# Two layers of attention and gated mixing on one core: a third buffer for values, another order of projections at an even pace, and later weights' maxima and splits over more steps

## The chip, the cores and the metric

The kernel runs on one core of a Trainium2 chip. The core has five engines that work at the same time, each in the order of its own instruction stream: PE (TensorE, matrix products), DVE (VectorE), ACT (ScalarE), POOL (GpSimd) and SP (SyncE), whose queue here issues nearly all DMA transfers. They wait for each other through semaphores. The metric is the device time of one execution in microseconds (us); the median of three runs of the kernel before is 2376.07 us (2370.62 to 2380.80).

## The reference

Two layers, each an attention block A with a residual and a gated block B with a residual, run twice with the same weights. The sequence has 2048 rows of 640 columns, 32 heads of 20 columns, and 4 segments of 512 rows.

```python
# block A, x is the normalized input; phi(t) = t + 1 if t > 0, else exp(t)
q, k, v = x @ wq, x @ wk, x @ wv            # split into heads and segments
for s in range(4):
    p = softmax(q[s] @ k[s].T * scale + causal mask)
    a_dot = p @ v[s]
    a_mem = phi(q[s]) @ M / (phi(q[s]) @ z + 1e-6)
    outs.append(g * a_mem + (1 - g) * a_dot)
    M, z = M + phi(k[s]).T @ v[s], z + sum(phi(k[s]))
x = x + concat(outs) @ wo
# block B, x normalized again
z1, z2 = split(gelu(x @ w_in)); z2 = layernorm(z2)
x = x + (z1 * (w_sp @ z2 + b_sp)) @ w_out
```

## The kernel before

**Precision.** Products are exact to about fp32: each fp32 operand is scaled by a power of two and split into a high and a low fp16 part (`split_scaled`: an ACT instruction, line 84, for the high part, a DVE instruction, line 85, for the low one), and a product is three fp16 matmuls (high by high, high by low, low by high). The power of two comes from the largest magnitude in the matrix. For the weights needed later (wo, both halves of w_in, w_out) `other_scales` brings them from memory in 32 pieces (line 182), reduces each on DVE (line 184), transposes the column maxima on PE, and forms the scales in `pow2_max` and `pow2_spread` (lines 58 to 77, 195 and 196). `Weight.load` then brings a weight piece by piece once more, splits it, and stores both parts to memory (line 128). In the second layer these weights are made already, and `load` only brings the stored parts.

**Phases.** Per layer there are phase 1a (attention, `Attention.run`), phase 1b (output projection of the last rows, normalization, w_in; line 308) and phase 2 (mixing along the sequence and w_out). In layer 0's phase 2 the head of layer 1's attention is woven in (`early`).

**The attention loop.** Heads are taken in pairs, 16 pairs to a segment, 64 in all. A pair takes three steps, so that there are 192 steps (0 to 191), a lead of 10 before them and some behind; a segment is 48 steps. At each step `scores` forms a chunk of the scores twice on PE: once for the row maxima of a pair two ahead (tile `mp`, reduced on DVE at line 1248) and once, with the maxima already subtracted, for the exponentials (tile `es`, read by ACT at line 1241 into `P`). `cast` turns `P` into a high part on ACT (line 1258) and a low part on POOL (line 1259). `pvs` multiplies them by the values (line 1285), and `combine` divides and adds the memory's share. `maxes` transposes the row maxima on PE and sends them through DMA into rows of the operand tile `qk` (line 1271). `read` and `update` read and write the memory M.

**Dense work.** Between those run the projections, called dense work here: `value(t)` makes the values of 128 rows (30 matmuls, line 1009; ACT line 1014 and DVE line 1015 write them to the value tile), `unit(s, m)` makes queries and keys of one of five groups of heads of segment s (30 matmuls, line 1066), and `project(t)` makes 128 rows of the output projection (30 matmuls, line 1042). `prep(t)`, the preparation of 128 rows, loads and normalizes them (lines 208 to 211 and 988), splits them (ACT line 223, POOL line 224), and transposes them by DMA; it is issued 11 steps before the value that needs it.

**What sets the order.** PE's order is that of the program. `order` is a list of the dense work: `v4` is a value tile, `12` unit 2 of segment 1, `p3` an output tile. Each has a nominal PE time in ns (6480 for a unit, 4530 for the others), and `PACE` says how many ns of it may run per step from which step on; the function `step` turns accumulated work into steps. Background work (`background`: the maxima, then wo and the second half of w_in) is a generator that yields the step at which it is to go on; the streams are merged step by step, and what preparations and background issue is held behind the newest attention instruction of ACT, DVE and SP. Weight pieces are staged in the pool `abg`, which has two buffers.

**Values.** A value tile holds a segment's values, high and low part with a column of ones (128 x 4 x 32 x 41 fp16). There are two, segment s in tile s % 2, so a value of segment 2 cannot be written before the products of segment 0 are done.

## Time and profile before

| | |
|---|---|
| median of 3 runs | 2376.07 us |
| the profiled execution, its span | 2378.28 us, 2376.6 us |
| PE busy | 2189.4 us, 92% of the span |
| DVE busy | 1500.2 us, 63% |
| ACT busy | 1173.3 us, 49% |
| POOL busy | 983.8 us, 41% |
| attention loop, layer 0 (steps 0 to 191) | 112.4 to 644.8 us |
| attention loop, layer 1 | 1326.4 to 1831.1 us |

How to read it: PE is matmul, PEld the load of its weights, SPq an instruction of SP's queue. A row of a group gives line, engine, operation, the tile written <- the tiles read, the count, busy time and the mean in ns of one, and then the idle time of the engine ahead of it with what ended it. A row of waits reads "who <- for whom: total us, times, longest us". A row of the timeline gives start, duration, engine, line, operation and tiles. A row of a stretch gives start and end, length, busy time and count of each engine, the clock that PE was granted (1.00 is full), the busy share of the DMA engines and GB/s. A wait for several things is put down to the one that came last.

### The profile page before, as it was taken

Reading aid. Unit: us, or ns where it says so; the run is one execution under the profiler, and the core shown is the slowest. Engines: PE = TensorE matmul, PEld = TensorE weight load, DVE = VectorE, ACT = ScalarE, POOL = GpSimd, SP = SyncE. Lnnn points to the kernel's source line nnn. Section 1 sums busy time; section 2 is a strip of 40 time slices with the busy share of each in tenths; the row PEclk is TensorE's granted clock in tenths of the full one; section 3 lists DMA queues with packets and bytes.
Section 4 is the critical chain, followed back from the end, with each engine's and each line's share of the span. In section 5 each row is a group of like instructions: output and inputs, shape, how many; then the busy total and the mean of one; then the engine's idle time right before and its main releaser. Section 6 shows DMA issues by size and latency. Waiting matters only on the chain. (4 is left out here: it accounts for less than half of the span.)

```text
span 2376.6 us, 50474 instructions
## 1 busy us (share of the span) xinstructions
PE 2189.4 (92%) x20490; PEld 1304.8 (55%) x20490; DVE 1500.2 (63%) x2790; ACT 1173.3 (49%) x1452; POOL 983.8 (41%) x773
## 2 busy tenths in 40 slices
PE   5878899899899979999998889999998999999998
PEld 2445555556545535555554555656565555555655
DVE  7678868877754543544314678787766668545454
ACT  3278678877632221212112698887676334322221
POOL 2078678888710100100001598888777323000000
PEclk9999899999999989999999999999999999999999
DMA  5653535455553477976633436454453534887875
GB/s 158 161 145 97 131 102 139 111 157 131 148 161 100 112 228 196 231 210 178 184 72 113 90 86 173 106 132 102 123 165 107 145 87 110 250 216 185 221 205 123
DMA packets 509418, 350.17 MB, mean 147 GB/s; under 512 B 409280, under 2 KB 444224, under 8 KB 504064
## 3 DMA queue, kind: packets, MB, share of 16 engines
q1 hardware_dynamic: 509184, 346.93, 55.7%
q8 instruction: 161, 2.64, 0.5%
q14 instruction: 73, 0.60, 0.1%
HBM read 160.83 MB, written 97.93 MB: 109 GB/s over the span
## 5 line engine op out<-in xcount | busy, mean ns | idle before, releaser
L1259 POOL TENSOR_TENSOR PL<-P,PH 128x1280 f16<-128x1280 f32 x248 | 650.1, 2623 | 117.2 <-ACT PH L1258 106.4
L1248 DVE TENSOR_REDUCE mx<-mp 128x2 f32<-128x1024 f32 (+3 forms) x512 | 408.8, 817 | 106.9 <-PE mp L1204 105.4
L1241 ACT ACTIVATE P<-es,sc 128x1024 f32<-128x1024 f32 (+1 forms) x384 | 370.7, 965 | 142.5 <-PE es L1204 140.6
L1258 ACT CAST PH<-P 128x1280 f16<-128x1280 f32 x256 | 320.4, 1253 | 19.9 <-PE pv L1285 10.5
L308 PEld LDWEIGHTS <-th 128*128 128x128 f16 x1920 | 188.2, 98 | 172.8 <-issue 10.2
L662 PE MATMUL gp<-zh,wt 128*128 128x432 f16 x1024 | 235.5, 350 | 15.3 <-DMA wt<-wn 15.3
L662 PEld LDWEIGHTS <-wt 128*128 128x128 f16 x1536 | 151.3, 99 | 149.0 <-DMA wt<-wn 17.7
L1232 PEld LDWEIGHTS <-qk 60*128 60x128 f16 (+1 forms) x2048 | 91.4, 94 | 229.9 <-issue 157.6
L211 POOL TENSOR_TENSOR lnrs<-lnve,mhalf 128x1 f32<-128x1 f32 x92 | 56.7, 625 | 382.4 <-DVE lnve L210 379.9
L461 PEld LDWEIGHTS <-wt 128*128 128x128 f16 x1344 | 131.5, 98 | 112.6 <-DMA wt<-wn 0.2
L1232 PE MATMUL mp<-qk 60*128 60x512 f16 (+3 forms) x1024 | 138.8, 308 | 42.6 <-DVE mx L1248 41.6
L1232 PE MATMUL es<-qk 64*128 64x512 f16 (+3 forms) x1024 | 135.7, 301 | 37.4 <-ACT P L1241 25.4
L1204 PEld LDWEIGHTS <-big 64*128 64x128 f16 x3072 | 141.9, 96 | 51.2 <-issue 4.0
L1285 PE MATMUL pv<-vs,PH 128*128 128x41 f16 x2560 | 167.8, 183 | 2.1 <-DVE ab L1301 2.0
L1009 PE MATMUL vps<-wvh,xt 128*128 128x320 f16 x640 | 155.8, 310 | 13.9 <-DMA xt<-xnhl 11.9
L1285 PE MATMUL pv<-vs,PL 128*128 128x41 f16 x2560 | 163.8, 181 | 1.6 <-POOL PL L1259 1.6
L1285 PEld LDWEIGHTS <-PH 128*128 128x128 f16 x2560 | 142.6, 96 | 18.5
L308 PE MATMUL zp<-wi1h,th 128*128 128x432 f16 x640 | 149.0, 347 | 0.6 <-DMA th<-xnhl 0.6
L1285 PEld LDWEIGHTS <-PL 128*128 128x128 f16 x2560 | 143.4, 97 | 4.2 <-POOL PL L1259 2.1
L662 PE MATMUL gp<-zl,wt 128*128 128x432 f16 x512 | 137.3, 350 | 0.0
L1066 PE MATMUL kps<-xt,wkh 128*128 128x512 f16 x380 | 122.8, 393 | 9.2 <-DVE phl L1100 9.1
L1009 PEld LDWEIGHTS <-xt 128*128 128x128 f16 x960 | 91.4, 101 | 54.2 <-DMA xt<-xnhl 12.9
(248 smaller groups left out, 4342.1 us busy)
## 6 DMA issues: line engine op xcount, KB each, us to landing
wr<-in_B_w_sp_dram SPq DMA_DIRECT2D x32, 1024.0 KB
qk<-st SPq DMA_DIRECT2D x256, 120.0 KB
x<-x SPq DMA_DIRECT2D x56, 320.0 KB
z<-z SPq DMA_DIRECT2D x32, 432.0 KB
cz<-z SPq DMA_DIRECT2D x32, 432.0 KB
turned<-wt SPq DMA_DIRECT2D x24, 512.0 KB
wt<-turned SPq DMA_DIRECT2D x24, 512.0 KB
st<-qhl SPq DMA_DIRECT2D x40, 256.0 KB
```

The costliest lines, as they stand in the source:

```text
L308: nc.tensor.matmul(zp[:, n, :FHH], a[:, k, :], b[:, k, c:c + FHH], start=(k == 0 and j == 0), stop=(k == KD - 1 and j == 2))
L461: nc.tensor.matmul(o[:, :FHH], wt[:, x, m, :], zb[b][:, y, m, :], start=start and i == j == 0, stop=i == NP - 1 and j == 2, skip_group_che ...
L662: nc.tensor.matmul(gp[:, n, :FHH], wt[:, k % 2, a, k // 2, :], b[:, k, n * FHH:(n + 1) * FHH], start=(k == 0 and j == 0), stop=(k == NT - ...
L1009: nc.tensor.matmul(ps, a[:, k, c], b[:, k, n * 320:(n + 1) * 320], start=(i == 0), stop=(i == 14))
L1066: nc.tensor.matmul(ps, a[:, k, c], b[:, k, :], start=(i == 0), stop=(i == 14))
L1204: nc.tensor.matmul(out, g.big[r, 64 - 64 * s:192 - 64 * s], mk, start=False, stop=s == 1, skip_group_check=True)
L1232: nc.tensor.matmul(out[:, h, o:o + w], a[r, ac], b[r, bc], start=o == 0, stop=False, skip_group_check=True)
L1241: self.last_of["ACT"] = nc.scalar.activation(P[:, :, 512 * c:512 * c + ew], es[:, :, :ew], AF.Exp, scale=g.esc).ins
L1248: self.last_of["DVE"] = nc.vector.tensor_reduce(self.mx[m][:, :, i], mp[:, :, o:o + w], AX.X, ALU.max).ins
L1258: nc.scalar.copy(PH, P[:, h])
L1259: (nc.gpsimd if h == 0 or n < self.N - self.TAIL else nc.vector).tensor_tensor(PL, P[:, h], PH, ALU.subtract)
L1285: nc.tensor.matmul(pv[:, i, h, :], x[:, c:c + 128], v[:, j, h0 + h, :], start=(j == 0 and x is PH), stop=(j == i and x is PL), skip_group_ ...
```

## The change

Five edits, all in the attention phase:

- A third value tile (`self.vs[2]`, in a new pool). Segment s uses tile s % 3. Values of segment 2 can be written while segment 0 is read.
- Another `order`: the values of segment 2 (v8 to v11) are put between the units of segment 1 (between 10 and 14), those of segment 3 (v12 to v15) between the units of segment 2, and the first output tile p0 behind unit 24; p1 to p3 come one unit earlier.
- Another `PACE`: 960 ns per step from step 0 and 1050 from step 60 to the end, in place of 700 from step 0, 1150 from step 53 and 1250 from step 128. The dense work then ends at step 196.9 instead of 190.4.
- The maxima of the later weights: a piece every 1.7 steps from step -8 (0.75 before); the last steps of their reduction at 50, 56 and 62 (50, 51 and 53 before).
- The splits: wo from step 72 with 3 steps between a load and its split (55 and 1.3 before), the second half of w_in with its first split at step 108 and 3.5 steps between (69 and 3 before).

A bookkeeping set (`spent`) and an assertion come with it and issue nothing.

```diff
@@ other_scales
-    yield 51
+    yield 56
     dg = pow2_max(g, pool, psum, tag, g.wam, 3, 4)
-    yield 53
+    yield 62
     pow2_spread(g, psum, tag, dg, 3, 4)
@@ Attention.__init__
-        self.xt, self.vs = [self.xt, None], [self.vs, None]
+        self.xt, self.vs = [self.xt, None], [self.vs, None, None]
@@ value
-            def out(ps=ps.rearrange("p (h d) -> p h d", d=DH), v=self.vs[s % 2][:, t % 4, n * 16:(n + 1) * 16, :]):
+            def out(ps=ps.rearrange("p (h d) -> p h d", d=DH), v=self.vs[s % 3][:, t % 4, n * 16:(n + 1) * 16, :]):
@@ update, pvs
-        v = self.vs[s % 2]
+        v = self.vs[s % 3]
@@ run
-        PACE = (-LEAD, 2400), (0, 700), (53, 1150), (128, 1250), (END + G, 0)
-        order = "02 03 v4 04 v5 v6 v7 10 11 12 13 14 v8 v9 v10 v11 20 21 p0 22 23 24 v12 v13 v14 v15 30 31 p1 32 p2 33 p3 34 p4 p5 p6 p7 p8 p9 p10 p11".split()
+        PACE = (-LEAD, 2400), (0, 960), (60, 1050), (END + G, 0)
+        order = "02 03 v4 04 v5 v6 v7 10 v8 11 v9 12 v10 13 v11 14 20 21 v12 v13 22 v14 23 v15 24 p0 30 p1 31 p2 32 p3 33 34 p4 p5 p6 p7 p8 p9 p10 p11".split()
...
-                assert s < 2 or beg > G * (s - 1) + self.LV + 3, (i, beg)
+                assert s < 3 or beg > G * (s - 2) + self.LV + 3, (i, beg)
...
-                    yield -8 + 0.75 * i if _ is True else _
+                    yield -8 + 1.7 * i if _ is True else _
                 nc.sync.dma_start(g.bsp, self.b_sp.rearrange("(t p) -> p t", p=128))
-            yield 54
-            for j, (w, width, pace) in enumerate(((g.wo, D, 1.3), (g.wi[1], FHH, 3))):
+            yield 70
+            for j, (w, width, at, pace) in enumerate(((g.wo, D, 72, 3), (g.wi[1], FHH, 108, 3.5))):
                 w.tiles(g.top[j])
                 for i, _ in enumerate(w.load(self.bg, width, "bg")):
-                    yield 55 + 14 * j + pace * i
+                    yield at + pace * i
...
         g = self.g
+        self.vs[2] = values_tile(g, self.pool("avs", 1))
```

More of the change, by code (lines that the diff above doesn't have):

```diff
@@ L831, in __init__ @@
         self.last_of = {}
+        self.spent = {(0, 0), (0, 1)}
     def post(self, k, f, free=False):
@@ L858, in setup @@
         g, nc, tc = self.g, self.nc, self.tc
-        pool = lambda n, b, **k: ctx.enter_context(tc.tile_pool(name=n, bufs=b, reuse_waits="tile", **k))
+        pool = self.pool = lambda n, b, **k: ctx.enter_context(tc.tile_pool(name=n, bufs=b, reuse_waits="tile", **k))
         sk, self.p3, self.pl2 = pool("ak", 1), pool("a3", 2), pool("al2", 2)
@@ L987, in norm @@
             mv, rs = ln
+            assert s < 2 or self.spent.issuperset((s - 2, m) for m in range(NU)), t
             nc.vector.tensor_scalar(xt, xt, mv[:, 0:1], rs, ALU.subtract, ALU.mult)
@@ L1069, in unit @@
             self.out(nm, s, m, ps)
+        self.spent.add((s, m))
     def out(self, nm, s, m, ps):
@@ L1279, in pvs @@
         pv = self.pv[n]
-        v = self.vs[s % 2]
+        v = self.vs[s % 3]
         for i in range(4):
```

## The prediction

> **What bounds the kernel now.** I read, in this order: the page's span, busy time by stretch, the waits of the stretches that stand out, the timeline around the longest, and the groups for prices. The attention loop runs 192 steps per layer, three exponentials (L1241) per pair of heads, so counting L1241 tells the step.

> ```profile
> 112.40:232.90 120.50, 46.19 (x48) 0.96 0.48 122
> 232.90:321.90 89.00, 23.14 (x24) 0.86 0.55 134
> 321.90:644.80 322.90, 115.90 (x120) 0.99 0.50 129
> ```

> These are L1241 alone: start and end, length, ACT busy and its count, granted clock, DMA share, GB/s. They cut layer 0 into A (steps 0 to 47), B (48 to 71) and C (72 to 191). All instructions in the same stretches, then layer 1's A, B and C:

> ```profile
> core 0: us, PE busy (x) PEld busy (x) DVE busy (x) ACT busy (x) POOL busy (x), PEclk, DMA share, GB/s
> 112.40:232.90 120.50, 99.92 (x1495) 61.03 (x1494) 98.40 (x187) 97.45 (x124) 93.40 (x54) 0.96 0.48 122
> 232.90:321.90 89.00, 72.88 (x863) 47.67 (x861) 67.46 (x133) 58.46 (x77) 64.72 (x45) 0.86 0.55 134
> 321.90:644.80 322.90, 303.52 (x4255) 195.14 (x4256) 251.33 (x492) 253.40 (x316) 264.51 (x182) 0.99 0.50 129
> 1326.40:1435.80 109.40, 96.33 (x1495) 59.61 (x1494) 87.64 (x166) 97.04 (x124) 93.09 (x54) 1.00 0.35 88
> 1435.80:1504.40 68.60, 61.54 (x862) 40.55 (x860) 56.73 (x116) 53.81 (x72) 61.05 (x45) 1.00 0.63 173
> 1504.40:1831.10 326.70, 308.30 (x4255) 196.89 (x4254) 245.41 (x484) 248.87 (x307) 265.57 (x183) 0.97 0.48 123
> ...
> 112.40:177.40 65.00, 50.48 (x739) 31.76 (x737) 52.04 (x100) 47.51 (x62) 44.87 (x26) 0.92 0.56 143
> ```

> Both layers run the same matmuls (1495, 863 or 862, 4255), yet layer 0's B is 20.4 us longer than layer 1's and its A 11.1 us. The difference is the background work that only layer 0 does. C is bound by PE (94% busy in both); A is bound by nothing alone: in layer 1 PE 88%, ACT 89%, POOL 85%, DVE 80%. The last row is the first 24 steps of layer 0, 2.7 us each.

> The waits of layer 0's B, then two of its A, then the one of layer 1's A:

> ```profile
> ACT P L1241 <- PE es L1204: 15.4, 8, 6.1
> PE mp L1232 <- DVE mx L1248: 6.2, 7, 1.3
> PE es L1232 <- ACT P L1241: 6.0, 4, 2.9
> ACT woh L84 <- DMA wst<-in_A_wo_dram: 4.7, 3, 1.9
> ACT wi1h L84 <- DMA wst<-in_B_w_in_dram: 3.5, 1, 3.5
> PE wtp L58 <- DVE mr L1269: 2.3, 1, 2.3
> ```

> ```profile
> PE mp L1232 <- DVE mx L1248: 13.4, 13, 2.4
> DVE wap L184 <- DMA wmst<-in_B_w_in_dram: 5.4, 6, 1.6
> ```

> ```profile
> PE mp L1232 <- DVE mx L1248: 5.1, 10, 1.6
> ```

> In B, ACT waits in order for weight pieces that have not landed, the exponentials queue behind it, and PE waits for them. The reduction of the maxima adds a transpose (L58) that PE meets right behind the one of the row maxima. In A, DVE waits in order for the pieces whose maxima it takes, and the scores wait for DVE. The timeline shows the two worst places, on DVE, SP and ACT:

> ```profile
> 242.21 2.38 DVE L62 TENSOR_SCALAR wdg<-ident,wmx 4x4 f32<-4x4 f32 x1
> 250.09 2.35 DVE L196 TENSOR_SCALAR sc<-pw 128x2 f32<-128x2 f32 x1
> ```

> ```profile
> 303.88 0.40 SPq L128 DMA_DIRECT2D w_oh<-woh  x1
> 304.33 0.42 SPq L128 DMA_DIRECT2D w_ol<-wol  x1
> 304.79 0.92 SPq L123 DMA_DIRECT2D wst<-in_B_w_in_dram  x1
> ```

> ```profile
> 313.27 0.65 ACT L84 ACTIVATE wi1h<-wst,iv 128x432 f16<-128x432 f32 x1 [3.46 <-DMA wst<-in_B_w_in_dram]
> ```

> Two tiny DVE operations take 2.4 us each. The first piece of the next weight is issued behind the store of the finished one (1.6 MB) and lands 8.5 us later, with ACT standing before it for 3.5.

> **The change, part by part.** The sum is made against the profiled execution: 2378.3 us, of which the span is 2376.6. It is 2.2 us above the median of the three runs, so I take 2 off at the end.

> *Dense work (projections of values, queries, keys, outputs).* Its nominal PE time is written in the code: 4.53 us for a value or output tile, 6.48 for a unit. Rows for size, from the chain, and for what goes along:

> ```profile
> 1498.17 2.14 PE vps L1009 x15
> 1671.39 2.27 PE kps L1066 x10
> ```

> ```profile
> L1014 ACT ACTIVATE vs<-vps 128x320 f16<-128x320 f32 x64 | 28.0, 440 | 30.0 <-PE vps L1009 29.7
> L1015 DVE SCALAR_TENSOR_TENSOR vs<-vps,vs 128x320 f16<-128x320 f32 x64 | 30.5, 479 | 34.8 <-ACT vs L1014 34.8
> L988 DVE TENSOR_SCALAR xt<-xt,lnmv,lnrs 128x640 f32<-128x640 f32 x28 | 29.8, 1072 | 1.9 <-POOL lnrs L211 1.8
> L208 DVE BATCH_NORM_STATS2 lnst<-xt 128x6 f32<-128x320 f32 x56 | 24.4, 479 | 6.9 <-DMA xt<-x 6.8
> L224 POOL TENSOR_TENSOR xnhl<-xt,xnhl 128x640 f16<-128x640 f32 x28 | 40.2, 1436 | 65.3 <-ACT xnhl L223 62.2 <-PE mtp L1266 2.3 <-DMA qk<-st 0.8
> L1259 POOL TENSOR_TENSOR PL<-P,PH 128x1280 f16<-128x1280 f32 x248 | 650.1, 2623 | 117.2 <-ACT PH L1258 106.4
> L184 DVE TENSOR_REDUCE wap<-wmst 128x1 f32<-128x432 f32 (+1 forms) x31 | 20.6, 670 | 10.3 <-DMA wmst<-in_B_w_in_dram 6.7 <-DMA wmst<-in_B_w_out_dram 2.7 <-DMA wmst<-in_A_wo_dram 0.8
> ```

> Thirty value matmuls at 0.143 us are 4.3; thirty of a unit at 0.227 are 6.8, so the nominal units hold within 6%. By the paces, the dense work of A goes from 48 x 0.70 = 33.6 to 48 x 0.96 = 46.1 us (+12.5), B from 25.3 to 24.1 (-1.2), C from 56 x 1.15 + 62.4 x 1.25 = 142.4 to 120 x 1.05 = 126.0 (-16.4), and behind step 191, where there was none, stand 4.9 steps (+5.1). Nothing is added or removed. What moves into A are the values v8 to v10 and the preparations of v8 to v11; the third place for values lets them be written while segment 0 is still read.

> Layer 1, A: PE 96.3 + 12.5 = 108.8 us. At A's own PE share of 0.88 this takes 123.6 us, at C's 0.944 it takes 115.3; its density, 0.96 per step, lies halfway from A's 0.70 to C's 1.19, so I take 0.914: 119.0, **+9.6**. B: -1.2 at 0.90, **-1.4**. C: -16.4 at 0.944, **-17.4**. Behind step 191: between 0 (PE waits there for the last products anyway) and 5.4; **+3**. Layer 1: -6.2.

> Layer 0, A: here DVE decides. It has layer 1's 87.6, three values (6 x 0.479 = 2.9), four preparations (each 2 x 0.479 + 1.07 + some 0.34 of small ones, so 9.5), and the maxima. These are 32 pieces, of which at 1.7 steps apart 27 fall into A: 27 x 0.67 = 18.1. Together 118.1 us. At 0.82 (98.4 of 120.5, A now) this takes 144.6; the best share of DVE that I find over ten steps is this one, 0.905, and gives 130.5:

> ```profile
> 387.00:423.00 36.00, 32.15 (x420) 18.41 (x417) 32.59 (x63) 29.92 (x39) 30.49 (x22) 0.96 0.56 138
> ```

> Between them: a piece is now reduced 0.75 step (2.0 us) behind its issue, then 1.7 (over 4 us), so DVE's waits for pieces go (5.4 us above, and 2.7 for the last weight in L184's row). 98.4 of 120.5 - 8.1 is 0.875, which gives 135.0: **+14.5**. Ahead of step 0 seven maxima fewer, 4.7 us of DVE beside a chain of projections: 0 to -4, **-2**.

> Layer 0, B: of its 20.4 us excess over layer 1, wo's splits (five, to steps 72 to 99) and the first of wi1 leave it altogether; the reduction stays, at steps 56 and 62 for 51 and 53. Step 56 has no transpose of row maxima before it, as step 51 has, so the 2.3 us before L58 go; the two DVE operations of 2.4 us stay. Layer 1's B would be 67.2; I add 4 for them and get 71.2, **-17.8**. Bounds: 67.2 (-21.8), or the whole excess of B's first 12 steps stays, 9.5 us (42.2 us in layer 0, 32.7 in layer 1, by L1241), giving 76.7 (-12.3).

> The clock is 0.86 in this stretch and 1.00 in layer 1's, 12.5 us of its 89, although PE's longest wait in it is the 2.9 us quoted. [...]

> Layer 0, C: -16.4 at 0.94, -17.4. Six splits move in (0.65 to 0.83 us of ACT each, less than 1.1 on DVE) where ACT and DVE are 78% busy: hidden, as long as each piece has landed. A split now comes 3 or 3.5 steps (8 us) behind its issue instead of 1.3. The store of wo still has the first piece of wi1 behind it, at step 99, but that one is split at 108; what remains is the fetches of queries and keys and the rows of maxima queued on SP behind 1.6 MB. Between 0 and the 3.5 us above; **+3** with wi1's own, larger store at step 174. So **-14.4**. Behind step 191: PE idles more there than in layer 1; **+1.5**. Layer 0: -2 + 14.5 - 17.8 - 14.4 + 1.5 = -18.2.

> The preparations that go into A hold a DVE scalar operation (L988, 1.07 us on average) beside a POOL that is 85% busy with L1259. [...]

> Also without price: the memset of the third place (POOL, 128 elements a partition, once per layer ahead of step 0), covered by the start, where POOL is idle; and the first tiles of the next phase, whose normalization runs inside layer 1's loop and stalls it. The new tile takes room that was free, so this may come later; I keep its cost.

> ```profile
> 1620.04 2.89 DVE xn L217
> ...
> 1693.98 2.31 DVE xn L217
> ```

> **Sum:** 2378.3 - 18.2 - 6.2 = 2353.9, against the median 2352. Ends: with the good bounds layer 0 gives -4 + 10 - 21.8 - 17.4 = -33 and layer 1 5.9 - 1.4 - 17.4 = -13, so 2330; with the bad ones layer 0 24.1 - 12.3 - 10 + 5 = +7 and layer 1 14.2 - 1.4 - 12 + 5 = +6, so 2389.

> **The rivals.**
> *A absorbs the moved work.* PE, ACT and POOL idle 11 to 15% there, so the 12.5 us could fill holes: A +6 or less in layer 1, +10 or less in layer 0, as in the good bounds: about 2334. For it: PE's waits in layer 1's A are many and short (5.1 us in 10). Against: no engine has much left.
> *A stretches by as much as C shrinks.* Both A at their present shares, +24.1 and +14.2, the rest as forecast: 2369. For it: nothing in A changes the order in which PE meets late scores.
> *B keeps its excess.* If it hangs on the reduction at 56 and 62, its two DVE operations and the clock they cost, more than on the splits: 9.5 instead of 4 stays, and 6 follow the splits into C: 2363 to 2368.
> *Slower.* One mechanism: DVE, in order, falls behind in A, scores wait for maxima (the 13.4 us above), and the clock falls with them, as in the first 24 steps now (clock 0.92). To be 0.5% slower both A together must grow by 48 us, all that B, C and the rest give back, and 12 more: from 230 to 290 us, 9.1 us a pair of heads where they take 7.2. The worst eight pairs now take 8.1 (65.0 us). That would be 2388 or more; its point is a DVE share of 0.75 or less.

> **How the numbers follow.** The forecast, 2352, has 0.42; full absorption 0.2; A stretching 0.15; B keeping its excess 0.08; slower 0.15. Half a per cent (12 us), about what a measurement of this kernel can tell, puts the bounds at 2364 and 2388. The forecast and absorption are faster, nearly all; the two rivals in the middle are mostly within: 0.63 faster, 0.21 the same, 0.16 slower. The range 2328 to 2386 leaves out under one in ten on the fast side, where only the good ends add up, and about one in ten on the slow side. The forecast's own range is 2340 to 2364.

> **What would show it.** Layer 0's B near 71 us with a clock over 0.95, and no wait of ACT for a piece over 1 us anywhere in the loop. A longer in both layers, 135 and 119 us, with PE over 0.9 in layer 1 and DVE near 0.87 in layer 0. C about 309 in both. L184 no longer waiting for DMA. Wrong if A in layer 0 passes 145 us, if the clock falls below 0.95 in a stretch where it was 1.00, or if C shrinks by less than 10 us.

## The result and the profile after

The changed kernel takes 2388.1 us (median of 8 runs, 2381.9 to 2391.5), the kernel before beside it 2374.4: 1.0063 times as long, 95% interval 1.0045 to 1.0082. It is 0.6% slower. The forecast was 2352, 1% faster, with 2386 as the upper end.

The profiled execution took 2381.9 us (span 2380.2), the lowest of its eight runs, while that of before is some 4 us above its own median. So the two profiles differ by 3.6 us where the medians differ by 13.7; some 10 us of the loss is in no profile shown here. The runs of one kernel lie 3 to 23 us apart (23.3 at most, in the run bgown below).

The six stretches after, all instructions, as the prediction shows those of before (PE, PEld, DVE, ACT, POOL busy, granted clock, DMA share, GB/s):

```profile
112.00:250.40 138.40, 111.49 (x1569) 69.44 (x1568) 110.53 (x217) 101.58 (x131) 97.41 (x59) 0.95 0.50 131
250.40:318.20 67.80, 61.66 (x849) 38.20 (x845) 53.12 (x110) 51.95 (x68) 55.34 (x38) 0.97 0.36 95
318.20:644.50 326.30, 296.21 (x4160) 189.33 (x4157) 254.06 (x487) 255.10 (x318) 270.79 (x185) 0.97 0.52 135
1337.40:1455.10 117.70, 105.24 (x1568) 65.80 (x1567) 95.59 (x190) 99.96 (x131) 97.65 (x59) 1.00 0.38 99
1455.10:1524.00 68.90, 62.72 (x847) 38.35 (x843) 50.13 (x100) 51.66 (x68) 55.32 (x38) 0.95 0.36 95
1524.00:1835.00 311.00, 292.84 (x4160) 187.81 (x4156) 240.21 (x472) 245.96 (x303) 265.42 (x185) 0.98 0.52 136
```

Length of each stretch, before to after, beside what was forecast ("behind 191": from the loop's end to the first quarter of phase 1b's matmuls):

| | layer 0 | forecast | layer 1 | forecast |
|---|---|---|---|---|
| A | 120.5 → 138.4, +17.9 | +14.5 | 109.4 → 117.7, +8.3 | +9.6 |
| B | 89.0 → 67.8, -21.2 | -17.8 | 68.6 → 68.9, +0.3 | -1.4 |
| C | 322.9 → 326.3, **+3.4** | **-14.4** | 326.7 → 311.0, -15.7 | -17.4 |
| behind 191 | 52.9 → 63.3, **+10.4** | **+1.5** | 49.2 → 52.1, +2.9 | +3 |

The remaining pieces (start, phase 2, the end) differ by -2.7 together. Layer 1 came as forecast, -4.2 for -6.2. Layer 0's A and B came within 3.5 us each. Two terms failed, both in layer 0: C by 17.8 us and the part behind the loop by 8.9.

**Layer 0's C.** Its first 24 steps, its middle and its last 24, and what follows the loop; first before, then after:

```profile
321.90:387.00 65.10, 62.10 (x858) 38.70 (x859) 51.18 (x102) 53.64 (x70) 50.95 (x36) 0.98 0.40 102
387.00:584.10 197.10, 187.23 (x2593) 118.91 (x2590) 155.48 (x302) 155.58 (x198) 166.51 (x116) 0.99 0.52 133
584.10:644.80 60.70, 54.19 (x816) 37.53 (x815) 44.67 (x90) 44.17 (x50) 47.05 (x32) 1.00 0.56 144
644.80:697.70 52.90, 47.74 (x297) 25.33 (x294) 30.51 (x59) 21.14 (x24) 14.16 (x15) 0.97 0.64 178
```

```profile
318.20:392.20 74.00, 62.03 (x863) 39.45 (x860) 60.84 (x119) 58.56 (x77) 62.26 (x44) 0.98 0.47 119
392.20:577.30 185.10, 177.97 (x2520) 112.40 (x2517) 147.63 (x282) 151.99 (x191) 161.37 (x109) 0.99 0.49 132
577.30:644.50 67.20, 56.20 (x787) 37.49 (x788) 45.59 (x88) 44.55 (x51) 47.16 (x34) 0.92 0.64 164
644.50:707.80 63.30, 55.06 (x335) 29.23 (x334) 31.20 (x61) 21.06 (x23) 13.53 (x15) 0.92 0.55 154
1524.00:1594.20 70.20, 62.10 (x859) 39.29 (x855) 57.40 (x116) 55.12 (x72) 60.74 (x45) 0.96 0.54 139
1779.10:1835.00 55.90, 52.66 (x787) 35.83 (x786) 38.45 (x75) 42.51 (x48) 43.92 (x31) 0.97 0.48 121
```

The middle shrank by 12.0. The first 24 steps grew by 8.9 although PE does the same there (62.1 and 62.0 us): DVE has 9.7 us more and POOL 11.3. Three of the four preparations of v12 to v15 now end there (their normalizations stand at steps 72, 75, 87 and 97, before at 102 to 114); that they are the cause is argued from this, no run isolates it. Layer 1 pays nearly as much (last but one row, +7.6; 62.6 before), without any splits, so this part does not come from the splits and is not what sets the two layers apart. The last 24 steps grew by 6.5 with 29 matmuls fewer; in layer 1 the same steps (last row) shrank, from 59.4 to 55.9. PE's waits in layer 0's last 24 steps:

```profile
PE es L1235 <- DMA qk<-mr: 4.4, 3, 3.0
PE mp L1235 <- DVE mx L1251: 3.1, 2, 1.6
PE yps L1044 <- DMA o<-o: 2.9, 2, 2.1
```

PE waits for transposed rows `o` of the output projection, which lie in the pool `abg`, the two buffers that w_i1's pieces pass through, now until step 174; and for rows of maxima that SP issues late. The store of w_i1 (2.2 MB) is issued in this stretch, at 599.3 us, but the row behind the longest of these waits is issued at 629.6, 30 us later, so the trace does not tie that wait to the store. The clock falls from 1.00 to 0.92.

**Behind the loop.** The first pieces of w_i0 are issued 8 us later, at the loop's end before and 8.3 us behind it after, and the first product with w_i0 comes 13.8 us behind the loop's end for 9.0 before. The row of SP's timeline before; then that of after, and from PE's timeline the first product with w_i0:

```profile
644.89 0.83 SPq L123 DMA_DIRECT2D wst<-in_B_w_in_dram  x2
```

```profile
652.81 0.81 SPq L123 DMA_DIRECT2D wst<-in_B_w_in_dram  x2
658.30 0.53 PE L308 MATMUL zp<-wi0h,th 128*128 128x432 f16 x2
```

The staging buffers of w_i0 lie, by address, over the transposed rows and the residual row of the last output tiles, so these pieces wait until the last output tile is done; the new pace lets it end behind step 191, 7.7 us behind the loop. The first product of phase 1b, with w_i1, stands right behind it, at 8.4 us (0.2 before). So two things are late there, the loads and PE itself; the runs pad and t190 below tell them apart.

### The profile page after: what moved, and what is told of

Same layout as the page of the kernel before. It is cut to its first block, busy times and chain, and to the rows that moved or that the text cites. A ratio compares the mean times of both kernels' runs of the same rounds, so it can differ in the third digit from the quotient of the medians.

```text
span 2380.2 us, 50487 instructions
## 1 busy us (share of the span) xinstructions
PE 2188.8 (92%) x20490; PEld 1299.6 (55%) x20490; DVE 1496.7 (63%) x2790; ACT 1171.9 (49%) x1452; POOL 985.6 (41%) x775
## 5 line engine op out<-in xcount | busy, mean ns | idle before, releaser
L308 PEld LDWEIGHTS <-th 128*128 128x128 f16 x1920 | 188.8, 98 | 174.3 <-issue 14.2
L662 PE MATMUL gp<-zh,wt 128*128 128x432 f16 x1024 | 235.9, 351 | 14.9 <-DMA wt<-wn 14.9
L211 POOL TENSOR_TENSOR lnrs<-lnve,mhalf 128x1 f32<-128x1 f32 x92 | 57.3, 631 | 400.5 <-DVE lnve L210 400.5
L1011 PE MATMUL vps<-wvh,xt 128*128 128x320 f16 x640 | 158.6, 312 | 33.1 <-DVE vs L1017 15.4
L662 PE MATMUL gp<-zl,wt 128*128 128x432 f16 x512 | 137.6, 351 | 0.0
```

What stands on the lines that cost most here:

```text
L308: nc.tensor.matmul(zp[:, n, :FHH], a[:, k, :], b[:, k, c:c + FHH], start=(k == 0 and j == 0), stop=(k == KD - 1 and j == 2))
L662: nc.tensor.matmul(gp[:, n, :FHH], wt[:, k % 2, a, k // 2, :], b[:, k, n * FHH:(n + 1) * FHH], start=(k == 0 and j == 0), stop=(k == NT - ...
L1011: nc.tensor.matmul(ps, a[:, k, c], b[:, k, n * 320:(n + 1) * 320], start=(i == 0), stop=(i == 14))
```

## The experiments

The edits below are shown shortened. All ratios are to runs of the kernel before on the same chip (medians 2371.6 to 2374.4 us). The lengths of the stretches in the profiles, in us, with "1" for layer 1:

| | ratio, interval | A | B | C | behind | A1 | B1 | C1 |
|---|---|---|---|---|---|---|---|---|
| before | 1 | 120.5 | 89.0 | 322.9 | 52.9 | 109.4 | 68.6 | 326.7 |
| changed | 1.0063, 1.0045 to 1.0082 | 138.4 | 67.8 | 326.3 | 63.3 | 117.7 | 68.9 | 311.0 |
| dense | 1.0113, 1.0094 to 1.0132 | 132.0 | 79.9 | 321.4 | 64.1 | 118.0 | 68.8 | 316.4 |
| maxb | 1.0008, 0.9994 to 1.0021 | 125.2 | 84.4 | 323.0 | 53.4 | 109.4 | 69.0 | 326.4 |
| bgonly | 1.0069, 1.0049 to 1.0088 | 125.1 | 76.5 | 340.9 | 52.2 | 109.5 | 72.6 | 325.9 |
| bgown | 1.0030, 1.0010 to 1.0049 | 127.9 | 76.9 | 331.2 | 52.6 | 109.4 | 74.5 | 328.2 |
| t190 | 1.0114, 1.0094 to 1.0134 | 141.6 | 66.4 | 333.9 | 55.4 | 117.7 | 68.9 | 327.7 |
| opool | 1.0041, 1.0027 to 1.0056 | 138.6 | 66.4 | 321.5 | 63.4 | 117.9 | 67.4 | 313.5 |
| pad | 1.0044, 1.0029 to 1.0059 | 139.2 | 67.8 | 320.9 | 58.0 | 118.0 | 70.2 | 313.7 |
| late | 1.0055, 1.0040 to 1.0070 | 138.0 | 68.8 | 325.4 | 63.7 | 117.7 | 70.3 | 313.7 |
| early | 1.0075, 1.0059 to 1.0092 | 139.3 | 67.8 | 335.1 | 58.0 | 117.8 | 67.4 | 315.0 |
| nosplit | 1.0060, 1.0036 to 1.0084 | 137.6 | 68.8 | 326.4 | 63.4 | 117.8 | 68.8 | 311.6 |
| third | 0.9989, 0.9976 to 1.0003 | 120.8 | 88.4 | 323.1 | 52.1 | 109.4 | 68.4 | 321.8 |
| touch | 1.0004, 0.9990 to 1.0019 | 120.3 | 86.8 | 324.2 | 51.8 | 110.4 | 69.5 | 323.9 |
| obtouch | 1.0000, 0.9987 to 1.0013 | 120.1 | 86.4 | 325.0 | 51.9 | 109.3 | 68.5 | 324.0 |
| bgb | 0.9994, 0.9982 to 1.0007 | 127.7 | 71.0 | 330.1 | 52.9 | 109.3 | 73.9 | 322.8 |
| best | 1.0029, 1.0014 to 1.0043 | 120.5 | 76.9 | 327.7 | 52.9 | 109.5 | 74.3 | 321.7 |

**The two halves of the change.** The new order without the spread background (dense, on the changed kernel):

```
-    yield 56  /  yield 62          (reduction of the maxima)
+    yield 51  /  yield 53
-  -8 + 1.7 * i
+  -8 + 0.75 * i
-  yield 70 ... (g.wo, D, 72, 3), (g.wi[1], FHH, 108, 3.5)
+  yield 54 ... (g.wo, D, 55, 1.3), (g.wi[1], FHH, 69, 3)
```

> The changed kernel with the times of the background work as before (maxima every 0.75 step, their reduction at 50, 51 and 53, splits from 55 and 69): third place, order and pace alone. Theory (spreading moved the background's cost, and added to it): layer 0 is longer than layer 1 by 27.7 us in the loop before and by 34.9 us after, so without the spreading the kernel is 5 to 9 us faster than the changed one, about 2381, with steps 48 to 71 of layer 0 back above 80 us and steps 0 to 47 near 130. Rival (the prediction's own): the spreading gives 18 us in steps 48 to 71 and costs less elsewhere, so without it the kernel is 10 us or more slower than the changed one, 2398 or more.

It measured 1.0113, 12 us slower than the changed kernel, the number of the rival. But the profile does not show the rival's gain: B is 12.1 us longer without the spreading, A 6.4 and C 4.9 shorter, layer 0's loop 0.8 longer in all. The rest of the profile's difference is 3.3 us ahead of step 0, where more of the maxima then stand, 5.6 in layer 1's loop, where the edit moves the fetches of the stored weights as well, and 9 in layer 0's phase 2, which the edit does not touch. So what the spreading is worth in the loop, beyond B, is not shown. The maxima alone (maxb), on the kernel before:

```
-  -8 + 0.75 * i
+  -8 + 1.7 * i
```

> The kernel before with one edit: a piece of the later weights every 1.7 steps instead of 0.75; nothing else. Theory (spreading moved the cost): each piece keeps its price, because DVE still waits for pieces that land late, and more of them fall into the loop (27 for 20), so steps 0 to 47 of layer 0 stay at 120 us or get longer, to 126, and the kernel is 0 to 6 us slower than before. Rival (the prediction's): the waits for pieces go, those steps fall to 115 or less, and the kernel is 5 us or more faster than before.

No difference in the time, as the theory had it: A +4.7 and B -4.6. The background of the changed kernel on the order of before (bgonly; wo's splits earlier than in the changed kernel, because the old order needs wo by step 85):

```
-  yield 51  /  yield 53  /  -8 + 0.75 * i
+  yield 56  /  yield 62  /  -8 + 1.7 * i
-  yield 54 ... ((g.wo, D, 1.3), (g.wi[1], FHH, 3)) ... 55 + 14 * j + pace * i
+  yield 56 ... ((g.wo, D, 57, 3), (g.wi[1], FHH, 108, 3.5)) ... at + pace * i
```

> The kernel before, with its order, pace and two places for values, and the background work of layer 0 nearly as the changed kernel has it: maxima 1.7 steps apart, their reduction at 56 and 62, w_i1's splits from 108 every 3.5 steps; wo's splits from 57 every 3 steps, since the old order needs wo by step 85. With the run of the new order alone (26 us slower than before) this is the fourth corner. Theory (wherever the background work is put it costs some 20 us of layer 0's loop, as the run with an earlier reduction showed): loop of layer 0 within 5 us of before, 2368 to 2377 us. Rival (the spreading itself gives the 12 us by which the changed kernel beats the run of the new order alone): the loop is 10 or more us shorter, 2358 to 2364 us.

Neither: 1.0069, slower. B gave back 12.5 us, but C grew by 18. Two pairs of heads carry 11.8 of that, pairs 55 and 57, steps 165 to 167 and 171 to 173: 14.0 and 13.0 us, where the kernel before takes 8.4 and 6.8. Their exponentials, then PE's timeline:

```profile
569.40:583.30 13.90, 2.87 (x3) 0.75 0.60 132
590.60:603.50 12.90, 2.86 (x3) 0.74 0.49 126
```

```profile
572.71 0.45 PE L1042 MATMUL yps<-woh,o 128*128 128x320 f16 x1 [3.24 <-DMA o<-o]
597.37 0.45 PE L1042 MATMUL yps<-woh,o 128*128 128x320 f16 x1 [3.95 <-DMA o<-o]
```

In both PE waits for `o`. The run that gives `o` buffers of its own (bgown):

```
+        self.ob = pool("aob", 2)
-        o = self.bg.tile([128, 2, KD, 128], F16, tag="bg", name="o")
+        o = self.ob.tile([128, 2, KD, 128], F16, tag="ob", name="o")
```

> The run of the spread background on the order of before (2386 us), with an own pool of two buffers for the rows that the output projection reads. Theory (pairs 55 and 57 of layer 0 take 14.0 and 13.0 us instead of 8.4 and 6.8 because the output projections wait for buffers held by w_i1's late pieces): both fall back to under 9, the loop of layer 0 is 9 to 12 us shorter, 2374 to 2378 us. Rival (the splits themselves cost it): 2383 to 2388 us.

The two pairs fell as expected,

```profile
571.30:579.50 8.20, 2.89 (x3) 1.00 0.66 178
586.90:593.80 6.90, 2.84 (x3) 1.00 0.40 82
```

with their clock back at 1.00. For these two pairs the mechanism is shown. But pairs 58 and 60 behind them took 11.7 and 11.1 us for 8.5 and 10.1, so C fell by 9.7, layer 0's loop by 6.5 (9 to 12 were expected) and the whole by 0.4%, which is still slower than before.

So by medians the order alone costs some 27 us, the background alone some 16, both together 15: each half is slower without the other. The profiles bear this out for the background alone (layer 0's loop is 10.0 us longer than before, no more than the two pairs make up), and not for the order alone.

**The output projection's own buffers, on the changed kernel** (opool; the same three lines):

> The changed kernel, with the output projection's operand tiles in two buffers of their own instead of the two that the weight pieces use as well. Theory (shared buffers): the splits of the second half of w_in now run until step 174 and hold the buffers that the output tiles need from step 121 on, so operands land late and PE waits for them (1.4, 2.2 and 0.7 us after step 160 in layer 0, none before the change), with the clock falling behind; with own buffers those waits go and steps 168 to 191 of layer 0 fall from 67 to 61 us, the kernel is 4 to 8 us faster than the changed one. Rival (the store of 2.2 MB at step 174): the waits for rows of maxima and the clock losses stay, and the gain is under 3 us.

As expected in kind: 1.0041 for 1.0063, 5 us, though the two intervals overlap, and C fell by 4.8; pairs 55 and 57 took 8.5 and 7.0 us for 9.3 and 10.3. The last 24 steps fell from 67.1 to 64.5 us only, not to 61.

**w_i1's store and splits.** First the store, placed behind phase 1b's ninth tile instead of behind the last split (late, with the own pool):

```
-        for t, d in ((self.h, self.kept[0]), ...): nc.sync.dma_start(d[:, :full], ...)
+        if self.nm != "i1": self.keep()
...
+            if i == 8 and w0 is None: g.wi[1].keep()
```

> The run with the own pool, and the store of w_i1 (its two split halves to DRAM) moved out of the loop of layer 0 to a place in phase 1b behind its ninth tile. Theory (pairs 59 to 61 of layer 0 are long because the fetches of the exponents' rows and of queries and keys queue behind this store): these three pairs fall from 30.6 us to about 24, the whole by 4 to 6 us, 2376 to 2378 us. Rival (they are long because the dense work left there is): under 2 us of difference, 2380 to 2384 us.

This tells nothing of the store, for it did not move out of the loop. SP's timeline of this run, then of the run it is made from:

```profile
584.38 0.32 SPq L136 DMA_DIRECT2D w_i1h<-wi1h  x1
```

```profile
591.54 0.39 SPq L128 DMA_DIRECT2D w_i1h<-wi1h  x1
```

It was issued 7 us earlier. Where a store stands in the program text does not decide when it is issued here. Then the splits at a faster pace (early, with the own pool and the pad below):

```
-  (g.wi[1], FHH, 108, 3.5)
+  (g.wi[1], FHH, 108, 2)
```

> The run with the own pool and the unused 1,344 bytes, and w_i1's splits every 2 steps from 108, so that they and their store end at step 148 instead of 174. Theory (layer 0's last eight pairs are longer than layer 1's because of w_i1's late splits and store): pairs 56 to 63 of layer 0 fall from 64 us to about 58, pairs 36 to 49 grow by less than 3, 2376 to 2379 us where the run it is made from took 2381.7. Rival (the work costs the same wherever it is put): 2380 to 2384 us.

Refuted, and the other way (1.0075). The end did not improve (the last eight pairs took 62.9 us in the run it is made from, not 64, and 62.7 here), and steps 129 to 146, where the splits now stand closer, paid for it; this run, then the run it is made from:

```profile
481.30:537.20 55.90, 17.37 (x18) 0.94 0.52 156
```

```profile
479.50:523.50 44.00, 17.35 (x18) 1.00 0.48 132
```

At last the changed kernel without these splits (nosplit):

```
+                if j and not w.made: w.fake()      # memset of both halves, store
```

> The changed kernel with w_i1's loads and splits left out of layer 0: its two halves are filled with zeros, stored, and fetched again as layer 1 fetches them, so the second half of the feed-forward's first product is computed from zeros. Theory (the splits and the two buffers that they share with the output projections are what keeps layer 0's C from shrinking as layer 1's does): C of layer 0 falls from 326.3 us to 306 to 312, my forecast for it, and the whole to 2368 to 2376 us. Rival (the denser preparations and the values there are the cause): C stays over 318 us.

C stayed at 326.4, as the rival had it, but the run does not test the rival's reason, because it is not clean. Steps 102 to 107 and 165 to 179, this run, then the changed kernel:

```profile
409.50:433.60 24.10, 5.85 (x6) 0.79 0.73 236
573.10:609.90 36.80, 14.47 (x15) 1.00 0.60 146
```

```profile
411.00:425.30 14.30, 5.80 (x7) 1.00 0.74 183
568.10:612.70 44.60, 14.48 (x15) 0.95 0.67 175
```

Without splits the late steps are 7.8 us shorter. Steps 102 to 107 are 9.8 longer: the stores of wo and of both halves of w_i1 are now issued one behind the other there (3.8 MB from 405.1 us on), and PE stands before a row of maxima, this run:

```profile
PE es L1242 <- DMA qk<-mr: 7.1, 1, 7.1
```

So by these profiles the late splits are worth about 8 of the 17.8 us. The run dense, whose splits end at step 126, agrees: it takes 37.7 us for steps 165 to 179. The median does not show it, 1.0060 for 1.0063, since the stores take it back.

**Behind the loop.** The dense work done by step 190 (t190):

```
-  (0, 960), (60, 1050), (END + G, 0)
+  (0, 960), (60, 1050), (100, 1135), (END + G, 0)
```

> The changed kernel with one number more in the pace: 1135 ns per step from step 100 on, so that the dense work ends at step 189.7 instead of 196.9; all else as in the changed kernel. Theory (the end of the loop): output tiles that are still in work behind step 191 keep the buffers in whose place the next phase stages its first weight, so in layer 0 that weight's loads start 8 us later; with the dense work ended before the loop the first matmul of the next phase comes within 2 us of the last exponential again (8.3 us now), and the kernel is 8 to 12 us faster than the changed one, about 2377. Rival (the late pace is right, PE bounds the loop's last part): the steps from 100 to 191 take as much longer as the end gains, and the time stays within 3 us of the changed kernel's 2388.

Behind the loop it is 55.4 us for 63.3, as expected of the place. But the loops grew by 9 and 17 us, and the whole is 12 us slower than the changed kernel, so neither the theory nor the rival held. Then room, and nothing else (pad, with the own pool):

```
+            pool("bpad", 1).tile([128, 336], F32, name="bpad")
             sp = pool("bs", 2)
```

> The run with the own pool for the rows that the output projection reads, and 1,344 bytes a partition left unused ahead of phase 1b's staging pool, so that the first pieces of w_i0 no longer lie where the last output tile's transposed rows lie. Theory (the 10 us behind layer 0's loop are the loads of w_i0, which wait for that room until the last output tile's matmuls end): the loads are issued at the loop's end or before, the first matmul of phase 1b with w_i0 comes 6 to 8 us sooner, 2374 to 2377 us. Rival (PE is late there because it still has the last tiles to project, whatever the loads do): within 3 us of the run with the own pool, 2379 to 2385 us.

The first two pieces are now issued in the loop, 38 us earlier than with the own pool alone:

```profile
607.09 0.96 SPq L123 DMA_DIRECT2D wst<-in_B_w_in_dram  x2
```

```profile
645.68 0.81 SPq L123 DMA_DIRECT2D wst<-in_B_w_in_dram  x2
```

Yet the first product with w_i0 came no sooner, 13.9 us behind the loop's end for 13.8; PE's timeline of pad, whose loop ends at 639.2:

```profile
653.07 0.53 PE L310 MATMUL zp<-wi0h,th 128*128 128x432 f16 x2
```

The first product of the phase stands at 8.4 us as without the pad, behind the last output tile. This is what the rival said. What came sooner stands behind it: what follows the loop fell from 63.4 to 58.0 us (58.0 in early too, which has the same pad), so half of the 10 us there is shown to be this overlap. The other half stays although the loads are early. The leftover dense work, 5.1 us by the pace, is of its size; with it done before the loop, loads and all, 2.5 of the 10 us are left (t190). The time did not follow the pad: 1.0044 for 1.0041. In the profile the loops are 1.4 and 3.1 us longer and phase 2 1.9; which of this is the pad's doing stays open.

**Layer 1's two stalls.** In C of layer 1, pairs 38 and 47 took 11.6 and 14.2 us before, 7.4 and 6.9 after; pair 50 took 7.0 and then 12.7. Before, then after:

```profile
1618.10:1629.70 11.60, 2.91 (x3) 0.85 0.33 74
1692.30:1706.50 14.20, 2.88 (x3) 0.76 0.25 62
```

```profile
1640.50:1648.00 7.50, 2.92 (x4) 1.00 0.28 90
1706.50:1713.40 6.90, 2.94 (x4) 1.00 0.44 121
1728.40:1741.10 12.70, 2.94 (x4) 0.87 0.71 179
```

The normalization of the next phase's first row tiles stands there. The kernel before with the third place allocated (third):

```
+        values_tile(g, self.pool("avs", 1))
```

> The kernel before with the third place for values allocated and cleared, and used by nothing. Theory (in layer 1 the first tiles of the next phase, whose normalization stalls the loop at pairs 38 and 47, lie in the room that the third place takes, so that they come later whoever uses the place): one of the two stalls goes, the loop of layer 1 is 4 to 5 us shorter, the rest is unchanged, 2368 to 2371 us. Rival (the stalls moved in the changed kernel by its order and pace): 2372 to 2377 us, pairs 38 and 47 as before.

No change (pairs 38 and 47: 11.6 and 13.2). But nothing in this program uses the tile once it is cleared, so the run does not show that its room was held. The same with a late write of one element (touch):

```
+        def touch():
+            yield 3 * G + 3
+            self.nc.vector.memset(spare[:, 0, 0, 0:1], 0.0)
```

> The kernel before with the third place for values allocated and cleared, and one element per partition of it written again at step 147, so that its room is held that long, as the changed kernel holds it. Theory (what moves layer 1's stalls at pairs 38 and 47 is that the next phase's third row tile lies in this room): pairs 38 and 47 fall from 11.6 and 14.2 us to about 7.5, pair 50 or a later one takes 12 to 13 instead of 7, layer 1's loop is 4 to 6 us shorter, 2366 to 2370 us. Rival (they moved by the new order and pace): pairs 38 and 47 as before, 2371 to 2377 us.

```profile
1617.50:1629.20 11.70, 2.92 (x4) 0.85 0.35 75
1691.50:1704.90 13.40, 2.89 (x4) 0.75 0.30 74
```

Again as before, so my theory of the room falls: the third place by itself neither costs nor gives anything. The stalls moved by the order or the pace; which, and why, stays open.

**Versions that might beat both.** On the kernel before, the reduction earlier and the splits later (bgb):

```
-  yield 50 / 51 / 53
+  yield 17 / 19 / 22
-  ((g.wo, D, 1.3), (g.wi[1], FHH, 3)) from 55 and 69
+  ((g.wo, D, 57, 3), (g.wi[1], FHH, 90, 2))
```

> The kernel before, with its order, its pace and its two places for values; only the background work of layer 0 is later or earlier: the reduction of the maxima at steps 17, 19 and 22 for 50, 51 and 53, the splits of wo from step 57 every 3 steps and of w_i1 from 90 every 2. The maxima stay 0.75 step apart. Theory (the 20.4 us by which layer 0's B exceeds layer 1's are the background's, and come back by its place alone, without the new order of the dense work): B falls from 89 to about 73 us, A and C gain 3 us each at most, the loop of layer 0 is 10 to 16 us shorter, layer 1 is unchanged, 2358 to 2364 us. Rival (the stall only moves: PE and ACT meet the same waits in A and C): loop of layer 0 within 5 us of before, 2370 to 2378 us.

B fell to 71.0 (the prediction had 71.2), but A paid 7.2 (steps 15 to 26, where the reduction now is) and C 7.2: no difference in the time. Pair 29 alone has 4.4 of C's. SP's timeline there, then PE's:

```profile
349.49 0.39 SPq L128 DMA_DIRECT2D w_oh<-woh  x1
349.93 0.42 SPq L128 DMA_DIRECT2D w_ol<-wol  x1
350.39 0.93 SPq L123 DMA_DIRECT2D wst<-in_B_w_in_dram  x1
351.36 2.98 SPq L1024 DMA_TRANSPOSE o<-o  x1
```

```profile
359.14 0.45 PE L1042 MATMUL yps<-woh,o 128*128 128x320 f16 x1 [4.00 <-DMA o<-o]
```

The transposed rows of the first output tile are now issued right behind the store of wo, and PE stands 4 us before them: the stall that ACT had in B came back on PE. The held third place with the own pool for `o` (obtouch):

> The run that holds the third place until step 147, on the kernel before, with an own pool of two buffers for the rows that the output projection reads. Theory (the output projections share two buffers with w_i1's splits in the kernel before too, until step 130): the loop of layer 0 is 2 to 4 us shorter than with the third place alone, 2363 to 2367 us, faster than both kernels. Rival (there is no such wait at the pace of before): the same as the run with the third place held, within 1.5 us.

The rival: 1.0000. At the pace of before, the sharing costs nothing that can be measured. And the parts that had looked free, together (best):

```
-  yield 51 / 53
+  yield 56 / 62
-  ((g.wo, D, 1.3), (g.wi[1], FHH, 3))
+  ((g.wo, D, 57, 3), (g.wi[1], FHH, 90, 2)), layer 1 as before, 4 steps more behind w_i1's first piece, own pool for o
```

> The kernel before with its order, pace and two places, and with the parts that gave time and no loss: the reduction of the maxima at steps 56 and 62, wo's splits from 57 every 3 steps, w_i1's from 90 and then every 2 steps from 96 (so that its second piece is not split behind the store of wo), layer 1's fetches where they were, and an own pool for the rows of the output projection. Theory (B is 12 us shorter, as in the run of the spread background, and C and A pay no more than 4): loop of layer 0 6 to 10 us shorter, layer 1 as before, 2362 to 2367 us, faster than both. Rival (the background costs the same wherever it is put): 2369 to 2376 us.

B fell by 12.1 and C grew by 4.8, most of it again at pair 29 (13.0 us); layer 0's loop is 7.3 us shorter, as expected. Its profile is 5.4 us shorter than that of before, its median 0.3% longer. The profile was the second lowest of 12 runs, which reach from 2369 to 2386. Here a single profile and the median disagree in sign, and nothing shown says where the slower runs spend it. No version is shown to beat the kernel before.

## Why the prediction was wrong, point by point

- **Ahead of step 0, -2.** Measured -0.4. The term itself is right: of the runs in the old order, those with a piece every 1.7 steps begin step 0 at 108.7 to 110.1 us (maxb, bgown, bgonly), those with 0.75 at 111.2 to 114.2. In the new order dense begins at 115.3, so something else there costs about as much.
- **Layer 0, A, +14.5: nearly the size, by errors that cancel.** "DVE's waits for pieces go" is false: they grew from 5.4 to 9.0 us for w_in's pieces and from 2.7 to 4.3 for w_out's. Behind them PE's wait for maxima grew from 13.4 to 14.9:

```profile
PE mp L1235 <- DVE mx L1251: 14.9, 15, 3.2
DVE wap L184 <- DMA wmst<-in_B_w_in_dram: 9.0, 7, 2.3
```

DVE's busy time came to 110.5, not 118.1 (layer 1's own grew by 8.0, not by 12.4: of the four preparations counted, A has only two more normalizations than before, since v11's falls at step 49 and an older one now stands ahead of step 0), and its share fell to 110.5 of 138.4, 0.80, where I had taken 0.875. A did stretch as DVE fell behind, but not to the 145 us that the prediction named as the sign of the slower rival. The four normalizations (L990, 128x640) in this A took from 0.59 to 2.89 us, 5.98 together where the sum had 4.3. L1259 has 79.1 of the 109.4 us of layer 1's A before, 72%; the prediction's 85% is all that POOL does there (93.09).
- **Layer 0, B, -17.8: the size and the wait are right,** -21.2, **the split of the sum is not.** The prediction gave 1.4 to the dense work and 16.4 to the background. The run dense has the order and pace without the spread background, and its B is 79.9: 9.1 by the order, 12.1 by the background. Three of the four preparations of v8 to v11 leave B (normalizations at steps 54 to 66 before, at 14, 26, 37 and 49 after), which the sum had added to A and not taken from B; that they are the 9.1 is not shown, for in layer 1 B stayed as it was. In the whole of layer 0's loop ACT now waits 0.7 us in all for weight pieces:

```profile
ACT woh L84 <- DMA wst<-in_A_wo_dram: 0.7, 2, 0.6
```

The clock of B rose from 0.86 to 0.97 with these waits gone. One other long wait of PE is left in it, until 279.3 us, and B's only fall of the clock, at 280.7, stands behind it:

```profile
PE vps L1011 <- DVE vs L1017: 3.7, 1, 3.7
```

- **Layer 0, C, -14.4: failed; it came to +3.4.** The step that failed is "-16.4 at 0.94, -17.4": it took 16.4 us less of PE work at one PE share for the whole of C, and one price, +3, for the background that moves in. PE's work did fall (95 matmuls), but its busy time by 7.3 us, not by 15.5 as in layer 1, since the clock of C fell from 0.99 to 0.97, that of its last 24 steps from 1.00 to 0.92 (at the clock of 0.50 at 613.5 us one 128x320 product of L1044 follows another after 0.27 us, at that of 1.00 at 605.5 us after 0.14); and PE's idle time grew from 19.4 to 30.1. In its place the profiles showed two terms, each from one profile of a kernel. The first 24 steps take 8.9 us more, by the preparations of v12 to v15 as far as the rows tell; I had counted those that move into A and not those that move from the middle of C to its start. The late splits of w_i1 are worth 8 (nosplit, and dense agrees), 4 of it by the two buffers shared with `o` (pairs 55 and 57 with an own pool), a resource that I did not list. These make 17 of the 17.8 us; the share of the store of w_i1 was not told apart, for the one run for it did not move it out of the loop.
- **Behind step 191, +1.5 in layer 0: failed; +10.4.** The step that failed is "PE idles more there than in layer 1", by which 5.1 us of dense work were to cost 1.5: with the loads out of the way (pad) 5.1 are left. The other 5.4 us are what waits for this work, the room of the last output tiles and with it the first weights of the next phase, which I had not listed; they are shown by the pad. In layer 1 the forecast +3 held, at 2.9.
- **Layer 1, A +9.6, B -1.4, C -17.4: right in size, C in part by luck,** +8.3, +0.3, -15.7. PE's share in A is 105.24 of 117.7, 0.894 for the 0.914 taken. In C 5.8 of the 15.7 come from the stalls above, whose cost I had kept; without them C gave about 10, not 17. The 7.5 that are missing are the size of the growth of its first 24 steps, 7.6, so this term was missed in both layers.
- **The rivals.** None describes what happened. "A stretches by as much as C shrinks" has A's growth too large and a shrinking of C that is absent in layer 0. The slower rival had the right sign and the wrong place: both A together took 256.1 us where it needed 290, and DVE in A was not what decided. I had no rival for buffers and room that two parts of the program share. Of the signs of being wrong that the prediction named, two came: the clock of 0.92 where it was 1.00, and layer 0's C, which did not shrink by 10 us.

## What to carry over

Before pricing work that moves to other steps, list what it holds there and until when: staging buffers, room of the next phase, a place in a queue. That a stretch is bound by PE says what PE's work is worth only while every stream that PE meets stays on time; price it by shorter pieces, and by what each moved preparation brings along. And where runs of one kernel spread by 10 us or more, a single profile that is 5 us shorter is no gain until the median says so.

## Of the hardware, not expected

In the changed kernel's last 24 steps of layer 0 the longest wait of PE is the 3.0 us shown above. The stretch at half clock at 611.8 us follows 3.4 us in which PE was busy for 40% and no idle time passed 1.51 us, behind 3.4 us in which it never stood still:

```profile
605.00:608.40 3.40, 3.40 (x58) 2.43 (x54) 1.47 (x3) 2.28 (x4) 3.32 (x3) 1.00 1.02 401
608.40:611.80 3.40, 1.36 (x14) 1.08 (x13) 2.60 (x7) 1.36 (x2) 1.93 (x2) 0.99 0.95 264
611.80:615.20 3.40, 3.34 (x35) 1.94 (x35) 1.67 (x4) 2.42 (x3) 1.27 (x3) 0.50 0.92 288
```
